# A gated mix of a long convolution and dilated attention: 114-query attention blocks, a second FFT stage in place, and whole-array weight loads

## The chip, the core and the metric

The kernel runs on one core of a Trainium2 chip. Five engines work side by side, each through its own instructions in order, and wait for one another on semaphores: TensorE (PE; its weight loads are listed apart as PEld), VectorE (DVE), ScalarE (ACT), GpSimd (POOL) and SyncE (SP, here the issuer of most DMAs). Matmul results go to PSUM, and VectorE or ScalarE copies them to SBUF. The metric is the device time of one execution in microseconds.

## What is computed

Inputs are bfloat16, with sequence S = 2048 and width D = 640. The same x (`A_q`) feeds a long convolution (a) and a windowed attention (b), mixed by a gate for each row.

```python
g = sigmoid((x * gate_w).sum(-1, keepdims=True))
# a: four-tap causal convolution of k, times v, then a 2048-tap causal convolution per channel
k_shift = sum(k_pad[:, t:t + S] * shift_k[:, 3 - t] for t in range(4))
kv = k_shift * v
a = x * (causal_conv(kv, ssm_k) + kv * ssm_D)          # by FFT of length 4096
# b: 32 heads of 20; a query at s sees the keys s, s-2, ..., s-14
q, k, v = split(x @ wqkv)
b = softmax(q . k_window * 20 ** -0.5) @ v_window @ wo
out = g * a + (1 - g) * b
```

## The kernel before

**Order.** The work is written as Python generators (`loads`, `conv`, `vproj`, `qkproj`, `score_gen` and so on), each of which yields requests for an engine with an estimated cost. A planner (`Plan.run`) picks among them by estimated start and priority while the program is built, and hands out four PSUM slots of two banks. The result is a fixed order of instructions on each engine; on the chip an engine never passes an instruction that waits.

**Attention.** Keys two apart have the same parity, so x is transposed (`transposes`) into `xT` with the even positions ahead of the odd ones, 1024 each, and the window becomes 8 neighbours. `vproj` (L440) makes the values `VW` for each block, with a 21st column of ones for the softmax's denominator. `qkproj` (L483) makes queries and keys for 128 features at a time in units of 10 matmuls; they are evicted to a staging tile `stg` (three buffers), and `fragger` (L524) sends the 20 rows of each head by DMA to row 32 x (head mod 4) of a set's tiles `qb` and `kb` (three of each; a set is four heads). Beneath the 20 feature rows lie 11 constant rows that add a large negative number to each score outside the window. A block is `BQ` = 57 queries against `BK` = 64 keys, 36 blocks. `score_gen` (L543) computes block scores with 31-row, 64-column tiles: two heads lie in each half of the 128 PSUM partitions. ScalarE takes the exponential (L567) into one of eight `ET` tiles, `pv_gen` (L587) multiplies by `VW`, and VectorE divides (L597, L601) into `oS`. Sets run t = 0 to 7.

**Convolution.** VectorE computes `kv` in 64 instructions of 1280 elements (L397 to L408). The long convolution is a four-step transform of 32 x 64 points: `s1h_unit` (L620) for the filter `h` and `s1u_unit` (L643) for kv are its first stage, `s2_unit` (L664) its second, with constants `F` and `G`. kv lies with 32 of its rows on each quarter of the partitions, so L643 works in 32x32 tiles with 64 columns. Stage 1 is evicted to `Am`, stage 2 from `Am` to `Hs` or `Up`. The channels run in `NG` = 5 groups of `IL` = 16 of every 80. VectorE multiplies the spectra (`mults`, L754 and L757: `Up` by `Hs`, and by `Hw`, which is `Hs` with its halves of partitions exchanged by DMA, `swaps`). `inverse1` (L771) and `final` (L856) are the inverse stages, through `Cm`.

**End.** `outproj` transposes `oS` into `oT` (L793) and multiplies by `wo` (L810) in tiles of 32 weight columns, four column groups side by side; the eviction scales by 1 - g into `bl`. `late_loads` reads x again into `qg` and the constants `T`; `qscale` (L836) multiplies by g. `final` runs twice, over groups 0 to 2 and then 3 and 4: VectorE multiplies the result in PSUM by `qg` (L863), adds `bl` (L867), and the output is stored in pieces of four rows to a partition block.

The two lines that set the sizes of a score and of an output matmul:

```python
nc.tensor.matmul(dst, lhsT=kb[r:r + DH + NF, BK * b:BK * b + BK], rhs=qb[r:r + DH + NF, BQ * b:BQ * b + BQ], ...
                 tile_position=(r, 64 * (rg // 2)))
nc.tensor.matmul(O[64 * sg:64 * sg + 64, half, c0:c0 + 21], lhsT=ET[64 * half:64 * half + 64, hl, BQ * (b % 8):BQ * (b % 8) + 64],
                 rhs=VW[64 * half:64 * half + 64, b, 2 * t + hl, :], ...)
```

Of the kernel before, what the change touches and what calls it, by code (L numbers as in the profile page):

```python
# [26 lines left out]
BQ = 57  # L27
BK = 64
NBP = 18
NB = 2 * NBP  # L30
PRE = 7
HS = 1024 + PRE
XW = 2072
# [4 lines left out]
OP = BQ * NBP  # L38
NET = 8


NG = 5
IL = 16
CR = 4

# [35 lines left out]
def attn_consts():  # L81
    B, C = 256.0, 512.0
    kk = np.arange(BK); qq = np.arange(BQ)
    kc = kk // 8 - 4; ko = kk % 8; qc = qq // 8 - 4; qo = qq % 8
# [19 lines left out]
def ccol(sb):  # L104
    return PRE + 128 * sb + (PRE if sb >= 8 else 0)
# [24 lines left out]
class Req:  # L130


    def __init__(self, engs, cost=0.0, deps=(), take=0, give=(), n=0, move=0.0, pri=None, mode=None, bg=None):
        self.engs, self.cost, self.deps, self.take, self.give, self.n, self.move = engs, cost, deps, take, give, n, move
        self.pri, self.mode, self.bg = pri, mode, bg
# [3 lines left out]
SWITCH = 110.0  # L139


class Plan:


    def __init__(self, nslots):
        self.at = dict(P=0.0, A=0.0, D=0.0, G=0.0, S=0.0, Q=0.0)
        self.mode = None
        self.pipe = 0.0
        self.lane = {"S": [], "G": [], "Q": []}
        self.slots = [Bank() for _ in range(nslots)]  # L150
        self.streams = []
        self.log = []
# [29 lines left out]
    def run(self):  # L182
        while self.streams:
# [13 lines left out]
            g.eng, g.banks = e, []  # L197
            g.done = Ev(end, e)
# [22 lines left out]
def kernel(  # L221
# [41 lines left out]
    kin = p0.tile([128, 35, 320], BF, name="kin", tag="H")  # L263
    kv = p0.tile([128, 32, 320], BF, name="kv", tag="kv")
    G = p0.tile([128, 32, 2, 128], BF, name="G")
    F = p0.tile([128, 384], BF, name="F")
    F1b = F[:, 0:128]
    M = F[:, 128:384].rearrange("p (a b) -> p a b", a=2)
    g_nat = p0.tile([128, 16], F32, name="g_nat")
# [4 lines left out]
    VW = pR.tile([128, NB, 16, DH + 1], BF, name="VW")  # L274
    ksets, qsets, ETs = [], [], []
    for e in range(3):
        kb = pR.tile([128, KW], BF, name=f"kb{e}")
        qb = pR.tile([128, QW], BF, name=f"qb{e}")
        ksets.append(kb); qsets.append(qb)
    for e in range(NET):  # L280
        ETb = pR.tile([128, 2, 8 * BQ + 8], BF, name=f"ET{e}")
        ETs.append(ETb)
    rd = pR.tile([128, 2, 12, 2], F32, name="rd")
# [4 lines left out]
    pa = pL.tile([128, CR, 320], BF, name="pa")  # L288
    wraw = pL.tile([128, 320, 4], BF, name="wraw", tag="pb")
    wl = pL.tile([128, 4, 320], BF, name="wl")  # L290
# [21 lines left out]
    st = {}  # L312
# [3 lines left out]
    def loads():  # L316
        def load(name, dst, src, us, deps=(), bg=None):
            g = yield Req("S", 500.0, deps, move=us, bg=bg, pri=None if bg is None else 6)
# [6 lines left out]
        def load_rows(name, dst, src, r0, r1, off):  # L325
            for rho in range(4):
                gg, ch = rho // 2, rho % 2
                lo = -3 if (r0 == 0 and off and gg == 1) else r0
                yield from load(f"{name}{rho}", dst[32 * rho:32 * rho + 32, lo + off:r1 + off, :],
                                raw(src, (32 * gg + lo) * D + 320 * ch, [[64 * D, 32], [D, r1 - lo], [1, 320]]),  # L330
                                (r1 - lo) * 32 * 640 / 200.0)
# [7 lines left out]
        yield from load_rows("kA", kin, k2, 0, 16, 3)  # L339
        yield from load("W0", Wqk[:, :, 0, :], W3[:, :, 0, :], 2400.0)  # L340
        yield from load_rows("vA", kv, v2, 0, 16, 0)
        yield from load("W1", Wqk[:, :, 1, :], W3[:, :, 1, :], 2400.0)
        yield from load_rows("kB", kin, k2, 16, 32, 3)
        yield from load_rows("vB", kv, v2, 16, 32, 0)
        wo = p0.tile([128, NDT, D], BF, name="wo", tag="wo")
        st["wo"] = wo
        yield from load("wo", wo[:], B_wo.rearrange("(t p) n -> p t n", p=128), 2400.0, [ev("vproj")], 500.0)
        for a in range(4):
            yield from load(f"G{a}", G[:, 8 * a:8 * a + 8], cf["G"].ap().rearrange("p (a r b) -> p a r b", a=32, r=2)[:, 8 * a:8 * a + 8],
                            1300.0, (), 500.0)  # L350
        h_lin = p0.tile([128, 80, 2, 64], BF, name="h_lin", tag="H")
        st["h"] = h_lin
        for c in range(2):
            for q in range(4):
                yield from load(f"h{q}{c}", h_lin[32 * q:32 * q + 32, :, c, :],
                                raw(A_ssm_k, (320 * c + 80 * q) * S, [[64, 32], [S, 80], [1, 64]]), 2100.0, [ev("conv")], 500.0)

    def heads():
        for c0, c1 in ((0, PRE), (HS, HS + PRE), (2 * HS, XW)):
            nc.gpsimd.memset(xT[:, :, c0:c1], 0.0)  # L360
        for ch in range(2):
            nc.gpsimd.memset(kin[32 * ch:32 * ch + 1, 0:3, :], 0.0)
        nc.scalar.dma_start(mm[:], ca["mm"].ap())
        for rho in range(4):
            nc.scalar.dma_start(wraw[32 * rho:32 * rho + 32], raw(A_shift_k, 1280 * (rho % 2), [[0, 32], [4, 320], [1, 4]]))
        for ch in range(2):
            for a, b in ((1, 17), (17, 32)):
                nc.scalar.dma_start(kin[32 * ch + a:32 * ch + b, 0:3, :],
                                    raw(k2, (64 * a - 3) * D + 320 * ch, [[64 * D, b - a], [D, 3], [1, 320]]))
# [3 lines left out]
        for q in range(4):  # L373
            nc.scalar.dma_start(Dz[32 * q:32 * q + 1, :], raw(A_ssm_D, 80 * q, [[0, 1], [320, 2], [1, 80]]))
        for e in range(3):
            nc.gpsimd.tensor_copy(ksets[e][:].rearrange("p (b k) -> p b k", k=BK), mm[:, 0:BK].unsqueeze(1).to_broadcast([128, NB, BK]))
            nc.gpsimd.tensor_copy(qsets[e][:].rearrange("p (b k) -> p b k", k=BQ), mm[:, BK:BK + BQ].unsqueeze(1).to_broadcast([128, NB, BQ]))
        nc.gpsimd.memset(VW[:, :, :, DH], 1.0)
        for o in (0, 64):
            for j in (0, NBP):  # L380
                nc.gpsimd.memset(VW[o:o + PRE, j, :, DH], 0.0)
        for e in range(NET):
            nc.gpsimd.memset(ETs[e][:], 1.0)
# [3 lines left out]
    def conv():  # L387
        yield Req("D", 1700.0, [Ev(12000.0)])
# [536 lines left out]
```

## Time and profile before

| | |
|---|---|
| median of 3 runs | 350.29 us (347.28 to 351.41) |
| the profiled execution | 352.19 us, of which the profile's span is 350.1 us |
| mean granted clock of TensorE in it | 0.817 |
| TensorE reads its first data | 6.9 us |
| first score matmul, first exponential | 62.5 us, 63.4 us |
| first matmul of the filter's transform (L620) | 165.0 us |
| first product of spectra (L754) | 217.8 us |
| projection (L810), first to last | 213.6 to 292.9 us |
| last VectorE instruction ends | 341.7 us |

All times below are microseconds from the start of the span. A row of the timeline or of the groups reads: line of the kernel, engine, operation, tile written, tiles read, shapes, count; in a timeline the start and the length stand ahead of it. The bracket or the last column says how long the engine had been idle just before and what ended that; "issue" is idle time in which the engine waited for nothing that the profile shows. In the slices each digit is a tenth of busy share (9 is 90% or more) and `PEclk` is the clock granted to TensorE in tenths. Matmuls are pipelined, so the durations of neighbours overlap; where the text speaks of a step, it is the distance between starts.

The largest idle times of the two engines that evict are ScalarE's 31.0 us for scores (L543) and 27.9 us for `pj` (L483), and VectorE's 38.0 us for outputs (L587).

### The profile page before, as it was taken

Reading aid. Unit: us, or ns where it says so; the run is one execution under the profiler, and the core shown is the slowest. Engines: PE = TensorE matmul, PEld = TensorE weight load, DVE = VectorE, ACT = ScalarE, POOL = GpSimd, SP = SyncE. Lnnn points to the kernel's source line nnn. Section 1 sums busy time; section 2 is a strip of 40 time slices with the busy share of each in tenths; the row PEclk is TensorE's granted clock in tenths of the full one; section 3 lists DMA queues with packets and bytes.
Section 4 is the critical chain, followed back from the end, with each engine's and each line's share of the span. In section 5 each row is a group of like instructions: output and inputs, shape, how many; then the busy total and the mean of one; then the engine's idle time right before and its main releaser. Section 6 shows DMA issues by size and latency. Waiting matters only on the chain. (4 is left out here: it accounts for less than half of the span.)

```text
span 350.1 us, 17133 instructions
## 1 busy us (share of the span) xinstructions
PE 251.0 (72%) x8158; PEld 198.0 (57%) x8158; DVE 176.1 (50%) x218; ACT 145.6 (42%) x172; POOL 24.7 (7%) x30
## 2 busy tenths in 40 slices
PE   2399999749599796465859788969979558445510
PEld 2278866646466464155748776947859436425510
DVE  0147699918574434113969552525434160996250
ACT  0235445604446354044767444736637424202200
POOL 9970000000000000001000000000000000000000
PEclk9999999958589898555787998998989977855855
DMA  7999964437323656173090000050501991000066
GB/s 202 272 217 221 220 139 102 84 107 195 108 75 81 126 103 108 31 132 63 7 222 22 5 6 4 4 124 4 123 5 33 235 203 78 6 4 2 4 152 150
DMA packets 39692, 34.78 MB, mean 99 GB/s; under 512 B 23246, under 2 KB 36552, under 8 KB 38472
## 3 DMA queue, kind: packets, MB, share of 16 engines
q1 hardware_dynamic: 38032, 31.82, 41.6%
q10 hardware_dynamic: 1592, 1.89, 2.5%
q8 instruction: 63, 1.03, 1.3%
q14 instruction: 5, 0.04, 0.0%
HBM read 20.26 MB, written 2.62 MB: 65 GB/s over the span
## 5 line engine op out<-in xcount | busy, mean ns | idle before, releaser
L483 PE MATMUL pj<-xT,Wqk 128*128 128x342 bf16 (+1 forms) x300 | 53.4, 340 | 2.3 <-issue 2.3
L567 ACT ACTIVATE ET<-sc 128x912 bf16<-128x912 f32 (+1 forms) x40 | 32.1, 853 | 31.2 <-PE sc L543 31.0
L483 PEld LDWEIGHTS <-Wqk 128*128 128x128 bf16 x300 | 30.4, 105 | 20.6 <-issue 2.4
L664 PE MATMUL s<-Am,G 64*128 64x64 bf16 x1280 | 30.3, 202 | 10.5 <-issue 8.2
L810 PE MATMUL op<-wo,oT 128*32 128x128 bf16 (+1 forms) x640 | 31.0, 349 | 8.2 <-issue 8.2
L664 PEld LDWEIGHTS <-G 64*128 64x128 bf16 x1280 | 25.8, 103 | 15.9 <-issue 12.0
L248 ACT CAST stg<-pj 128x684 bf16<-128x684 f32 (+1 forms) x25 | 19.0, 761 | 34.2 <-PE pj L483 27.9
L440 PE MATMUL psv<-Wv,xT 128*64 128x320 bf16 x360 | 28.1, 319 | 5.3 <-ACT xT L248 3.9
L248 ACT CAST Cm<-i 128x1024 bf16<-128x1024 f32 x17 | 17.2, 1012 | 26.2 <-PE i L771 26.1
L771 PE MATMUL i<-F,Hw 128*128 128x128 bf16 x160 | 24.0, 244 | 5.4 <-DVE Hw L757 5.4
L440 PEld LDWEIGHTS <-xT 128*64 128x64 bf16 x360 | 21.4, 117 | 11.0 <-ACT xT L248 4.4
L810 PEld LDWEIGHTS <-oT 128*32 128x32 bf16 x640 | 17.6, 142 | 17.0 <-issue 12.9
L754 DVE TENSOR_TENSOR Hs<-Up,Hs 128x2048 bf16<-128x2048 bf16 x10 | 12.2, 1222 | 27.2 <-ACT Up L248 27.1
L597 DVE RECIPROCAL rd<-O 128x48 f32<-128x48 f32 (+1 forms) x16 | 6.1, 383 | 38.4 <-PE O L587 38.0
L543 PE MATMUL sc<-qb,kb 31*64 31x57 bf16 x1152 | 17.9, 208 | 10.4 <-issue 5.8
L771 PEld LDWEIGHTS <-Hw 128*128 128x128 bf16 x160 | 21.9, 154 | 5.8 <-DVE Hw L757 5.6
L771 PE MATMUL i<-F,Hs 128*128 128x128 bf16 x160 | 24.4, 246 | 0.2 <-DVE Hw L757 0.2
L587 PE MATMUL O<-VW,ET 64*64 64x21 bf16 x1152 | 16.3, 191 | 10.7 <-issue 9.7
L543 PEld LDWEIGHTS <-kb 31*64 31x64 bf16 x1152 | 14.7, 124 | 16.1 <-issue 11.1
L643 PE MATMUL s1u<-F,kv 32*32 32x64 bf16 x1280 | 21.3, 217 | 3.5 <-issue 3.5
L771 PEld LDWEIGHTS <-Hs 128*128 128x128 bf16 x160 | 21.8, 153 | 1.4 <-issue 0.7
L643 PEld LDWEIGHTS <-kv 32*32 32x32 bf16 x1280 | 19.6, 144 | 5.2 <-issue 4.6
(55 smaller groups left out, 351.8 us busy)
## 6 DMA issues: line engine op xcount, KB each, us to landing
Hw<-Hs SPq DMA_DIRECT2D x10, 512.0 KB
xS<-in_A_q_dram SPq DMA_DIRECT2D x4, 640.0 KB
kv<-in_A_v_dram SPq DMA_DIRECT2D x8, 320.0 KB
h_lin<-in_A_ssm_k_dram SPq DMA_DIRECT2D x8, 320.0 KB
qg<-in_A_q_dram SPq DMA_DIRECT2D x4, 640.0 KB
kb<-stg SPq DMA_DIRECT2D x28, 90.0 KB
qb<-stg SPq DMA_DIRECT2D x28, 80.2 KB
G<-cf_G SPq DMA_DIRECT2D x4, 512.0 KB
```

The source lines that it names most:

```text
L248: nc.scalar.copy(dst, src)
L440: nc.tensor.matmul(ps[64 * o:64 * o + 64, i, 0:320], lhsT=xT[:, dt, s0:s0 + BK], rhs=rhs, start=(dt == 0), stop=(dt == NDT - 1), tile_posi ...
L483: nc.tensor.matmul(ps[:, i, 0:n], lhsT=Wqk[:, dt, w, 128 * ft:128 * ft + 128], rhs=xT[:, dt, s0:s0 + n], start=(dt == 0), stop=(dt == NDT ...
L543: nc.tensor.matmul(dst, lhsT=kb[r:r + DH + NF, BK * b:BK * b + BK], rhs=qb[r:r + DH + NF, BQ * b:BQ * b + BQ], start=True, stop=True, tile ...
L567: nc.scalar.activation(ETs[e][:, :, 0:BQ * nb], scs[k][:, :, 0:BQ * nb], ACT.Exp, scale=SCALE)
L587: nc.tensor.matmul(O[64 * sg:64 * sg + 64, half, c0:c0 + 21], lhsT=ET[64 * half:64 * half + 64, hl, BQ * (b % 8):BQ * (b % 8) + 64], rhs=V ...
L597: nc.vector.reciprocal(rv, Ov[:, :, :, :, DH])
L643: nc.tensor.matmul(pss[bank // 2][o:o + 32, bank % 2, 64 * k:64 * k + 64], lhsT=kv[rows, :, cp], rhs=F1b[rows, 64 * ch:64 * ch + 64], star ...
L664: nc.tensor.matmul(o, lhsT=G[rows, j, rr, :], rhs=Am[rows, 2 * j + rr, :, :], start=(rr == 0), stop=(rr == 1), tile_position=(64 * c, 0), ...
L754: nc.vector.tensor_tensor(Hs[:, c], Up[:, c], Hs[:, c], ALU.mult)
L771: nc.tensor.matmul(o, lhsT=src[:, c, :, :, 8 * oc + il].rearrange("p q j -> p (q j)"), rhs=M[:, k, :], start=(k == 0), stop=(k == 1), skip ...
L810: nc.tensor.matmul(op[32 * gg:32 * gg + 32, n0:n1], lhsT=raw(a, OP * (t % 2) + t // 2 + 8 * gg, [a.ap[0], [32, 32]]), rhs=wo[:, ft, n0:n1] ...
```

## The change

It rewrites most stages for fewer and larger matmuls. The number of matmuls, by line of before:

| | before | after |
|---|---|---|
| transposes of x (L420) | 80 | 80 |
| values (L440) | 360, 64-column weights | 180, 121-column weights |
| queries, keys (L483) | 300 | 300 |
| gate (L454) | 320 | 160 |
| scores (L543) | 1152, 57 columns | 576, 114 columns, 128-column weights |
| outputs (L587) | 1152 | 576 |
| stage 1 of h (L620) | 160 | 160 |
| stage 1 of kv (L643) | 1280, 32x32 tiles | 160, 64-row tiles with 128-column weights |
| stage 2 (L664) | 1280, 64 columns | 512, 160 columns |
| transposes of oS (L793) | 90 | 90 |
| projection (L810) | 640, 32-column weights | 160, 128-column weights |
| first inverse (L771) | 320 | 320 |
| last inverse (L856) | 1024, 96 or 64 columns | 512, 160 columns |
| all | 8158 | 3786 |

Attention blocks have 114 queries and 121 keys, 18 of them, and one head in a score tile; scores take two PSUM slots, and `stg` has two buffers.

```diff
-BQ = 57
-BK = 64
-NBP = 18
+BQ = 114
+BK = 121
+NBP = 9
+GROUPS = [[0, 1, 2, 3], [4, 5, 6, 7], [8, 9, 10, 11], [12, 13, 14], [15, 16, 17]]
+PARTS = [((0, 1, 2), 0, 2), ((3, 4), 12, 1)]
...
+            for gi, blocks in enumerate(GROUPS):
+                nb = len(blocks)
+                g = yield Req("P", 4 * nb * 28.0 + 30.0, [ev(f"set{t}"), ev("ET")], take=2, mode="s", mm=4 * nb)
...
+                for bb, b in enumerate(blocks):
+                    for rg in range(4):
+                        r = 32 * rg
+                        nc.tensor.matmul(scs[rg // 2][:, rg % 2, BQ * bb:BQ * bb + BQ], lhsT=kb[r:r + DH + NF, BK * b:BK * b + 128],
+                                         rhs=qb[r:r + DH + NF, BQ * b:BQ * b + BQ],
+                                         start=True, stop=True, tile_position=(r, 0), skip_group_check=True)
...
+                    nc.scalar.activation(st["ET"][0:BK, e, :, 0:BQ * nb], scs[k][0:BK, :, 0:BQ * nb], ACT.Exp, scale=SCALE)
...
+                                nc.tensor.matmul(O[:, (b - b0) // 6, c0:c0 + 21], lhsT=st["ET"][0:BK, e, hh, BQ * bb:BQ * bb + 128],
+                                                 rhs=VW[0:BK, b, 4 * t + h4, :], start=True, stop=True, skip_group_check=True)
...
-    CH = 6
+    NSTG = 2
```

kv is computed with 16 successive positions on each partition (instructions of 2560 elements), written to a tensor in memory, `kv_d`, and read back as `kvT`, so that both h and kv go through one first stage of 64 rows. `h`'s loads wait for the stores.

```diff
-    kv = p0.tile([128, 32, 320], BF, name="kv", tag="kv")
+    pv = p0.tile([128, 4, 2, 16, 80], BF, name="pv", tag="kv")
+    kv_d = dpool.tile([4, 128, 2, 16, 80], BF, name="kv_d")
...
+        for q in range(4):
+            yield from load(f"kvD{q}", kv_d[q].rearrange("p c n i -> p (c n i)"), pv[:, q].rearrange("p c n i -> p (c n i)"), 3000.0, [ev("conv")], 1500.0)
...
+    def s1_unit(key, P, oc, Am, free):
...
+                if key == "h":
+                    lhsT = st["h"][rows, i, :, :].rearrange("p c n -> p (c n)")
+                else:
+                    lhsT = st["kvT"][rows, :, :, i].rearrange("p c n -> p (c n)")
```

The channels run in two halves `P` instead of five groups. Stage 2 reads and overwrites the same tile (`Hs` or `U`); it can begin for a half only when stage 1 of that half is evicted. The first half of `h` needs no tile that attention holds, so its transform may begin during attention; the second half of kv reuses the tile of `oT` and follows the projection.

```diff
+    def s2_unit(j0, n, Am, deps):
+        r = yield Req("P", 4 * n * 34.0 + 30.0, deps + [ev(f"G{j // 8}") for j in (j0, j0 + n - 1)], take=1, mode="r", mm=4 * n)
...
+                    nc.tensor.matmul(ps[:, c, 160 * jj:160 * jj + 160], lhsT=st["G"][rows, j0 + jj, rr, :], rhs=Am[rows, :, 2 * (j0 + jj) + rr, :],
+                                     start=(rr == 0), stop=(rr == 1), tile_position=(64 * c, 0), skip_group_check=True)
...
+        copy(e.eng, Am[:, :, 2 * j0:2 * j0 + 2 * n, :].rearrange("p q (j c) l -> p c j q l", c=2),
+             ps[:, :, 0:160 * n].rearrange("p c (j q l) -> p c j q l", j=n, q=4))
...
+        yield Req("G", 1.0, [ev("outproj")])
+        U = p0.tile([128, 4, 64, PL], BF, name="U1", tag="H")
...
+            yield Req("S", 1.0, outs("h", P) + [ev("p3")] + ([ev("us1")] if P else []))
...
+                            nc.tensor.matmul(o, lhsT=src[:].rearrange("p q (j c) l -> p c l (q j)", c=2)[:, c, l + il, :], rhs=M[:, k, :],
```

The projection loads 128 weights at a time, the last inverse runs once over all 160 columns in groups of three rows (`m` = 3), and ScalarE copies its result to `yb` before VectorE multiplies and adds.

```diff
+                    nc.tensor.matmul(op[:, n0:n1], lhsT=oT[:, ft].rearrange("p h m a -> p a (h m)")[:, t, :], rhs=wo[:, ft, n0:n1],
...
+                nc.scalar.copy(yb[:, 0:m, 320 * k:320 * k + 320].rearrange("p n (q c) -> p q n c", q=2),
+                               pss[k][:, :, 0:160 * m].rearrange("p q (n c) -> p q n c", n=m))
...
+            nc.vector.tensor_tensor(reg, yb[:, 0:m, :], reg, ALU.mult)
...
+            nc.vector.tensor_tensor(reg, reg, bl[:, t0:t0 + m, :], ALU.add)
```

Inputs k and v are loaded in halves of 8 positions to a partition (10,240 bytes in a row), the taps on all 128 partitions, and one `ET` tile of eight parts is filled with ones after the first quarter of the convolution. The planner's costs get a term for each 256 instructions of TensorE (`PAGE`, `FETCH`); it changes the order, not the instructions.

## The prediction

> **What bounds the kernel now.** I read the page first (busy shares, slices, queues), then TensorE's timeline, then busy time by stage, then groups by form.
>
> ```profile
> PE 251.0 (72%) x8158; PEld 198.0 (57%) x8158; DVE 176.1 (50%) x218; ACT 145.6 (42%) x172; POOL 24.7 (7%) x30
> ...
> PE   2399999749599796465859788969979558445510
> ...
> PEclk9999999958589898555787998998989977855855
> ...
> q8 instruction: 63, 1.03, 1.3%
> ```
>
> TensorE is the busiest engine, 72% of the span, with holes from 60 us on, and its granted clock dips at the holes. The last line is the traffic of program code: 63 packets of 16 KB. TensorE has 16,318 instructions (8158 weight loads, 8158 matmuls, two branches); 256 to a packet makes 63.7. The timeline of TensorE in the last inverse transform shows what this does:
>
> ```profile
> 326.28 2.20 PE L856 MATMUL i<-Cm,T 32*32 32x64 bf16 x247 [1.10 <-ACT Cm L248]
> 330.54 1.29 PE L856 MATMUL i<-Cm,T 32*32 32x64 bf16 x128 [2.06 <-issue]
> 333.99 1.27 PE L856 MATMUL i<-Cm,T 32*32 32x64 bf16 x128 [2.17 <-issue]
> 337.75 0.26 PE L856 MATMUL i<-Cm,T 32*32 32x64 bf16 x9 [2.48 <-issue]
> ```
>
> Bursts of exactly 128 matmuls (256 instructions) run in 1.3 us and then wait for nothing else: one burst per 3.45 us (330.54 to 333.99), 27 ns a matmul where the array needs 10. My reading is that code arrives at 256 instructions per 3.45 us. Over all of TensorE's timeline "issue" waits come to 23.2 us from 62.5 to 165, 22.4 us from there to 298 and 10.3 us after: 56 us. By stage (columns: span, busy time and count of PE, PEld, DVE, ACT, POOL, clock, DMA share, GB/s):
>
> ```profile
> 16.00:62.50 46.50, 46.50 (x522) 34.63 (x519) 34.13 (x41) 21.75 (x31) 8.35 (x13) 1.00 0.91 181
> 62.50:165.00 102.50, 73.75 (x2817) 54.14 (x2816) 47.00 (x80) 43.21 (x56) 0.95 (x1) 0.73 0.49 102
> 165.00:298.00 133.00, 107.78 (x3655) 89.39 (x3652) 64.07 (x58) 73.18 (x78) 0.00 (x0) 0.87 0.31 71
> ```
>
> Projections fill the first stage at full clock. Attention, then the transforms, hold 2817 and 3655 matmuls; at 27 ns these need 76 of 102.5 us and 99 of 133 us for code alone. ScalarE comes next with 55% (73.18 of 133), so the code rate, with the low clock that its holes bring (0.73), is what these two stages are worth cutting for.
>
> **The change, stage by stage.** It issues 3786 matmuls: 7574 instructions, 102 us of code at 3.45 us per 256, spread over the whole span, so code stops being the bound everywhere but in the last transform.
>
> Prices that the trace has:
>
> ```profile
> L567 ACT ACTIVATE ET<-sc 128x912 bf16<-128x912 f32 x32 | 28.0, 928 | 20.8 <-PE sc L543 20.6
> L248 ACT CAST Cm<-i 128x1024 bf16<-128x1024 f32 x17 | 17.2, 1012 | 26.2 <-PE i L771 26.1
> L754 DVE TENSOR_TENSOR Hs<-Up,Hs 128x2048 bf16<-128x2048 bf16 x10 | 12.2, 1222 | 27.2 <-ACT Up L248 27.1
> 174.83 0.39 PE L620 MATMUL s<-F,h_lin 64*128 64x128 bf16 x8
> ```
>
> *To the first exponential (now 63.4 us).* ScalarE issues 10 loads ahead of its first copy instead of 15, so TensorE no longer stands until 15.8 us for xT; but its queue carries 0.69 MB more (taps on 128 rows, halo), 2.9 us at the 235 GB/s of the first 16 us, so Wv lands at 10.65 + 2.9 = 13.6 us. Then 60 transposes at 60 ns (3.6), 180 value matmuls at 136 ns (24.5: 1.36 us for 20 half-wide ones now, the same array time), 7 query/key units at 1.46 us (10.2) and 160 gate matmuls at 27 ns (4.3; the 320 of now take 10.7 us): 56.2, and 1 us for W0, now wanted earlier. **57 us.**
>
> *Attention (now 102.5 us).* Scores and outputs fall from 2304 matmuls to 1152. A score has a 128-column load and 114 columns on one of four row groups: bounds 12 ns (114 columns at the 0.42 ns of L483's 342 in 145, four abreast) and 64 ns (the 128x128 pairs of L771); nearest is L620 above, 8 matmuls with 128-column loads in 0.39 us, 27 ns apart once the pipe's 0.2 us is taken off. Outputs, 21 columns behind a full 128-column load: 11 (now) to 64, I take 35. So 15.6 + 20.2, 23 query/key units 33.6, and 9 us of first transforms: TensorE has 78 us. But ScalarE's exponentials double: 121 of 128 partitions hold one head where two shared them, so 48 of 912 columns and 32 of 684 replace 32 and 8. By the rows (0.928; 0.741 on the line through 0.554 at 456) that is 68.3 us, back to back (two in 1.75 us, a step of 0.82) 59.5; now 32.1. With 15 evictions of pj (11) and two of s1 ScalarE has 72 to 81 us and is the bound: I take 81, as its work mostly arrives in pairs.
>
> Waits on top: the convolution still takes 32 x 2 x 0.82 = 52 us of VectorE, from some 27 us (6.0 MB of loads up to k's first half at 225 GB/s) to 82 with the outputs of set 0 between. The new store of its product waits for that in SyncE's queue, ahead of the fragments for set 3, and two more 0.66 MB stores lie among them: at 220 GB/s the queries of the third feature block land near 92 us. With two staging buffers, not three, ScalarE's next eviction waits for these and blocks exponentials behind it, at about 85 us: 8 us. The same pair of buffers costs some 6 us in later sets (now 10.1 us of SyncE's waits on scores). Sum 81 + 14 = 95 us, to **152**. Bounds: 72 dense, 102.5 if nothing is won.
>
> *Transforms to the end of the projection (now 165 to 295).* The array needs 360 s2 matmuls at 35 ns (160/64 of 14 ns), 80 + 80 s1 at 27 and 45, 90 transposes at 56, 16 projection units at 1.4 (640 columns x 5 at 0.42 ns; four column groups abreast take 1.5 now), 160 L771 pairs at 64. Eviction bounds the first half: 30 on ScalarE at 0.9 (27 us, +2 for two barriers) against 21 on VectorE at 1.14 and 5 oT at 1.2 (30): **33 us**. Then TensorE has projection and inverse together, 22.4 + 10.2, at a clock near 0.9 **36 us**, covering VectorE's eight products (11.4) and bl (11.5). The strided weights (160-byte step, 32 now) are nowhere in the trace: 56 ns to twice 64 for L771 gives 32 to 43.
>
> *The last half (now 298 to 350 is 52).* It is serial: s1 for kv 7, meanwhile four swaps of 0.66 MB start only after its last matmul: 4.5 + 2.6 MB at 210 GB/s + 2 = 19, later than s2 (15). Then the products in 10, i1's last two units and a copy 4.5, code-and-VectorE-paced last transform 14.5 (11 products and sums at about 1.2, start and end), output 5 (8.4 us now for 1.3 MB behind the last sum; the last piece is 0.16 MB, behind 0.49 MB): **53 to 54**. Bounds 48 and 60.
>
> Sum: 57 + 95 + 33 + 36 + 54 = 275 us of span, and 2.1 outside it (352.19 against 350.1): 277 us. The profiled execution lies 1.9 us above the median of 350.29, inside the runs' 347.28 to 351.41; I leave it at 277.
>
> Done at no price: the ET fill (7 us on GpSimd, under the conv), the trip of kv to memory and back (2.6 MB each way, 12 us, under sets 5 to 7; if that cover is gone, up to 10 us before kv's s1), T and qg.
>
> Two rules stand against this. The Trainium skill, "Runtime: NRT & Kernel Launch", Instruction fetch mechanics, has the crossing of a 16 KiB block of code as mostly hidden; the four timeline rows with 2.1 to 2.5 us per block disagree, and by the page the 56 us would have another cause and stay, 333 us. "TensorE: Matmul & The Clock Gate", LDWEIGHTS, has 128 columns cost 107 ns a load, which would make the 1152 attention loads 123 us and the whole some 350; the row with 8 such loads in 0.39 us says a quarter.
>
> **Rivals.**
> - *Attention wins nothing* (102.5 us): doubled exponentials and blocked queues eat the code gain. For it: ScalarE runs in order and evicts pj between exponentials. 57 + 102.5 + 123 + 2 = 285, up to 308 with the upper bounds behind it.
> - *The stalls are not code* and stay with time: 277 + 56 = 333. Against: bursts of 128, and 63 packets.
> - *All dense*: 57 + 72 + 29 + 32 + 48 + 2 = 240 to 257.
> - *Slower: PSUM serializes attention.* There are four slots of two banks; a score group now takes two, outputs one, pj one. If exponentials, scores, outputs and pj of a set never overlap, a set costs 3 x 2.7 + 2 x 2.2 (scores, 0.25, two exponentials, 0.12), 3.7 + 2.2 for outputs and their division, and three pj units at 2.45: 25.8 us, eight sets 206, and the whole 388. It decides from 21.6 us a set, against 11.9 in my sum. For it: the first eight exponentials each wait for both slots; against: two slots stay for the other group whenever no pj or output is in flight.
>
> **Chances.** Forecast 0.60; attention wins nothing 0.19; dense 0.06; stalls stay 0.05; serialized 0.10, of which 0.02 come out within 1%. A change under about 1% can't be told from none here. Range 255 to 308, holding the first two cases. Faster 0.90, same 0.02, slower 0.08.
>
> **What would show it.** Code packets near 30 and "issue" waits of TensorE under 15 us, nearly all in the last transform; exponentials 60 to 68 us with few gaps between 57 and 152; ScalarE waiting for DMA on stg near 85 us; ScalarE and VectorE over 85% busy in the 33 us after attention; Hw late against U1. Wrong if the first exponential starts after 62, if a set takes over 15 us, or if L771's pairs with the new stride are over 100 ns apart.

## The result, and the profile after

The changed kernel takes 304.11 us, the median of 4 runs (302.72 to 305.58), beside 350.85 us for the kernel before (4 runs, 347.28 to 354.11): a ratio of 0.870, 95% interval 0.861 to 0.878. The time lies in the forecast range, 27 us above the forecast. The profiled execution took 305.58 us, 303.8 of it span. These lines of its page answer to those shown of before:

```profile
PE 231.9 (76%) x3781; PEld 185.7 (61%) x3786; DVE 172.5 (57%) x181; ACT 177.8 (59%) x217; POOL 24.5 (8%) x23
...
PE   0499999997988895994888979999999742984210
...
PEclk9999999859799799697555999999999795895555
...
q8 instruction: 29, 0.48, 0.7%
```

63 packets of code have become 29. TensorE is nearly full as far as the projection's end at 233 us, though with dips of its clock, and thin behind that. Busy time by stage (columns: span, busy time and count of PE, PEld, DVE, ACT, POOL, clock, DMA share, GB/s):

```profile
63.90:167.00 103.10, 84.74 (x1473) 56.38 (x1473) 49.78 (x67) 74.57 (x97) 0.94 (x1) 0.78 0.63 141
...
167.00:198.00 31.00, 27.63 (x611) 24.24 (x610) 29.18 (x29) 26.51 (x30) 0.00 (x0) 0.98 0.40 87
198.00:234.00 36.00, 35.69 (x327) 29.90 (x334) 16.87 (x25) 23.08 (x28) 0.00 (x0) 1.00 0.50 104
...
268.00:304.00 36.00, 9.96 (x545) 7.62 (x544) 12.56 (x12) 12.89 (x15) 0.00 (x0) 0.59 0.32 75
```

The last row is the sight to explain: 36 us in which no engine is busy for more than 13. By stage, in us of span:

| stage | before | forecast | after |
|---|---|---|---|
| to the first exponential | 63.4 | 57 | 63.9 |
| attention, to the last output matmul | 101.6 | 95 | 103.0 |
| transforms to the projection's start | } 133 | 33 | 31.0 |
| projection and first inverse, first half | } | 36 | 35.6 |
| the rest | 52.1 | 54 | 70.3 |

By these stages the whole gain came from the two in the middle (133 to 66.6); attention won nothing, and the last half lost 18 us. They do not hold the same work as before, though. Attention now also holds the start of the filter's transform (7.4 us of TensorE), and the last half holds the second half of kv's transform and half of the first inverse (25.0 us of TensorE, where 7.9 of such work stood before). A large part of what the last half lost is in ScalarE's timeline of the last transform:

```profile
277.04 0.88 ACTq L876 DMA_DIRECT2D out_dram<-qg  x2
277.97 1.82 ACT L866 CAST yb<-i 128x960 bf16<-128x960 f32 x2 [3.33 <-DVE qg L873]
282.20 0.86 ACTq L876 DMA_DIRECT2D out_dram<-qg  x2
283.16 1.82 ACT L866 CAST yb<-i 128x960 bf16<-128x960 f32 x2 [3.37 <-DVE qg L873]
```

Every 5.19 us ScalarE evicts a group of three rows (L866), then comes to the issue of that group's output DMAs (L876), which must wait for VectorE's sum (L873). The next group's evictions stand behind that issue: 3.4 us idle in each round. TensorE and VectorE in turn wait for the eviction, as the table of waits shows (us in total, times, longest):

```profile
DVE qg L871 <- ACT yb L866: 23.1, 6, 10.0
ACT yb L866 <- DVE qg L873: 16.8, 5, 3.4
...
PE i L859 <- ACT yb L866: 7.9, 5, 3.1
```

In the kernel before, VectorE multiplied out of PSUM itself, and none of the last transform's evictions stood behind ScalarE's DMA issues.

### The profile page after: what moved, and what is told of

It is laid out like the page before. It is cut to its first block, busy times and chain, and to the rows that moved or that the text cites. A ratio compares the mean times of both kernels' runs of the same rounds, so it can differ in the third digit from the quotient of the medians.

```text
span 303.8 us, 8436 instructions
## 1 busy us (share of the span) xinstructions
PE 231.9 (76%) x3781; PEld 185.7 (61%) x3786; DVE 172.5 (57%) x181; ACT 177.8 (59%) x217; POOL 24.5 (8%) x23
## 4 chain that ended last, share of the span: by engine, by line
PE 58%; DVE 17%; DMA 9%; ACT 6%; SPq 4%; issue 4%; ACTq 1%; DVEq 0%
PE pj L522 14%; PE i L777 9%; PE psv L476 9%; PE op L810 7%; PE O L617 5%; DVE U L269 5%; DVE Hs L269 4%; DMA Hw<-Hs 4%; DMA xS<-in_A_q_dram 3%; PE sc L589 3%; PE gps L494 3%; SPq L563 2%; PE s L669 2%; DMA kb<-stg 2%; DVE qg L871 2%
## 5 line engine op out<-in xcount | busy, mean ns | idle before, releaser
L597 ACT ACTIVATE ETall<-sc 121x912 bf16<-121x912 f32 (+1 forms) x80 | 63.4, 858 | 22.2 <-PE sc L589 21.9
L476 PE MATMUL psv<-Wv,xT 128*121 128x320 bf16 x180 | 28.7, 313 | 1.0 <-DVE xT L269 1.0
L269 DVE CAST U<-s 128x1024 bf16<-128x1024 f32 (+2 forms) x23 | 25.8, 1171 | 6.0 <-PE s L669 3.2
L589 PE MATMUL sc<-qb,kb 31*128 31x114 bf16 x576 | 20.2, 243 | 10.7 <-DMA kb<-stg 3.7
L267 ACT CAST stg<-pj 128x684 bf16<-128x684 f32 (+1 forms) x21 | 15.6, 745 | 18.7 <-PE pj L522 14.3
L476 PEld LDWEIGHTS <-xT 128*121 128x121 bf16 x180 | 24.9, 142 | 2.5 <-issue 1.2
L267 ACT CAST Hs<-s 128x960 bf16<-128x960 f32 (+1 forms) x25 | 23.1, 994 | 3.1 <-PE s L669 1.8
L269 DVE CAST Hs<-s 128x1024 bf16<-128x1024 f32 (+2 forms) x17 | 19.1, 1152 | 7.6 <-PE s L653 6.1
L810 PE MATMUL op<-wo,oT 128*128 128x512 bf16 (+1 forms) x155 | 22.6, 301 | 0.3
L267 ACT CAST VW<-psv 121x640 bf16<-121x640 f32 x18 | 12.5, 696 | 14.6 <-PE psv L476 14.6
L866 ACT CAST yb<-i 128x960 bf16<-128x960 f32 (+1 forms) x12 | 9.9, 873 | 18.0 <-DVE qg L873 16.8
L810 PEld LDWEIGHTS <-oT 128*128 128x128 bf16 x160 | 16.5, 147 | 5.9
```

The costliest lines, as they stand in the source:

```text
L267: nc.scalar.copy(dst, src)
L269: nc.vector.tensor_copy(dst, src)
L476: nc.tensor.matmul(ps[0:BK, n0 // 320, 0:320], lhsT=xT[:, dt, s0:s0 + BK], rhs=Wv[:, dt, n0:n1], start=(dt == 0), stop=(dt == NDT - 1))
L589: nc.tensor.matmul(scs[rg // 2][:, rg % 2, BQ * bb:BQ * bb + BQ], lhsT=kb[r:r + DH + NF, BK * b:BK * b + 128], rhs=qb[r:r + DH + NF, BQ * ...
L597: nc.scalar.activation(st["ET"][0:BK, e, :, 0:BQ * nb], scs[k][0:BK, :, 0:BQ * nb], ACT.Exp, scale=SCALE)
L810: nc.tensor.matmul(op[:, n0:n1], lhsT=oT[:, ft].rearrange("p h m a -> p a (h m)")[:, t, :], rhs=wo[:, ft, n0:n1], start=(ft == 0), stop=(f ...
```

## The experiments

All ratios are to the kernel before, timed on the same chip. "The changed kernel" is the 304 us one.

**Outputs issued by SyncE alone.**

```diff
-                (nc.sync, nc.scalar)[gg % 2].dma_start(raw(outf, ...
+                nc.sync.dma_start(raw(outf, ...
```

> The changed kernel, but all four output DMAs of a group of rows are issued by SyncE; before, two of four were issued by ScalarE. Theory: in the changed kernel's last transform ScalarE's DMA issue waits for VectorE's sum of that group, and as ScalarE works in order the next group's two evictions stand behind it; a group takes 5.19 us and the transform 28.8 us (271.7 to 300.5). With SyncE issuing, a group costs the largest of its code (96 matmuls, 0.75 of a 3.45 us packet, 2.6 us), ScalarE's two evictions of 960 elements (about 2 us) and VectorE's product and sum (about 2.4 us): 2.6 us a group, the transform 15 to 17 us, the whole 12 us less: about 292 us. Rival A, the transform is bound by code or by VectorE anyhow: a group stays near 5 us and the time within 3 us of 304. Rival B, eight DMA issues on one queue in place of two queues cost the gain back at the end: about 300 us.

297.21 us (4 runs, 295.91 to 298.72), ratio 0.845 (0.837 to 0.853), clear of the changed kernel's interval. ScalarE's and VectorE's timelines in the last transform now read:

```profile
281.23 3.55 ACT L866 CAST yb<-i 128x960 bf16<-128x960 f32 x4 [1.84 <-PE i L859]
285.36 2.48 ACT L866 CAST yb<-i 128x960 bf16<-128x960 f32 x4 [0.58 <-PE i L859]
```

```profile
285.36 1.15 DVE L871 TENSOR_TENSOR qg<-yb,qg 128x1920 bf16<-128x1920 bf16 x1
286.54 1.16 DVE L873 TENSOR_TENSOR qg<-qg,bl 128x1920 bf16<-128x1920 bf16 x1
287.62 1.15 DVE L871 TENSOR_TENSOR qg<-yb,qg 128x1920 bf16<-128x1920 bf16 x1
```

Evictions run four in a row, and VectorE goes at its own pace, 2.26 us a group. From the transform's first matmul to its last sum it takes 17.9 us, where it took 28.8. SyncE's 24 issues end 2.7 us behind the last sum, so the tail grew from 3.3 to 5.0 us; with a start 1.3 us later the span is 7.9 us shorter. The mechanism is shown; I had expected 12 us of it.

**Code in the kernel before: each score matmul issued twice.**

```diff
                             score(scs[sl][o:o + 64, rg % 2, BQ * k:BQ * k + BQ], rg, 16 * a + 8 * sl + k)
+                            score(scs[sl][o:o + 64, rg % 2, BQ * k:BQ * k + BQ], rg, 16 * a + 8 * sl + k)
```

> The kernel before, with every score matmul issued twice with the same operands into the same place, so 1152 matmuls and 1152 weight loads more, all in attention; the result is the same. Theory (TensorE's program code arrives at 256 instructions per 3.45 us and this bounds attention): 2304 instructions are 9 packets, 63 become 72, and attention gets up to 9 x 3.45 = 31 us longer: about 375 to 382 us. Rival, the stalls come from something else and the array's time counts: a score matmul of 57 columns is at most 11 ns busy beside others, 1152 x 11 = 13 us, part of it in holes: 350 to 363 us.

380.74 us (4 runs), ratio 1.081 (1.068 to 1.094). Its page:

```profile
q8 instruction: 72, 1.18, 1.4%
```

The scores' waits in it, and below them those of the kernel before:

```profile
PE sc L543 <- issue: 18.4, 12, 2.3
```

```profile
PE sc L543 <- issue: 5.8, 4, 2.0
```

Nine packets more, and a span of 376.1 in place of 350.1 us: 2.9 us a packet, near the 3.45 of the bursts. About half of it is in these waits, the rest in TensorE's busy time (251.0 to 266.8 us); the rival, the array's time alone, had allowed 13 us at most. The code rate did bound attention before. The Trainium skill, "Runtime: NRT & Kernel Launch", Instruction fetch mechanics, has the crossing of such a block as mostly hidden; these 26 us for nine blocks say otherwise.

**Attention: half of the exponential's columns.**

```diff
-... activation(st["ET"][0:BK, e, :, 0:BQ * nb], scs[k][0:BK, :, 0:BQ * nb], ACT.Exp, scale=SCALE)
+... activation(st["ET"][0:BK, e, :, 0:57 * nb], scs[k][0:BK, :, 0:57 * nb], ACT.Exp, scale=SCALE)
```

> The changed kernel, with each exponential taken over half of its columns only (57 a block in place of 114); the other half of the weights stays as it was, so part of the softmax is left out. The forecast had ScalarE as the bound of attention with 81 us of work out of 95. The 80 exponentials are 63.4 us now and would be about 36. Theory (ScalarE bounds attention): attention shortens by most of 27 us, the whole to 277 to 283 us. Rival A (attention stands on staging buffers, on fragment DMAs and on TensorE's order, ScalarE busy only 63 of 95 us): it shortens by 5 to 12 us, the whole to 292 to 299 us. Rival B (nothing but TensorE's order): within 4 us of 304.

305.15 us in one run: nothing won. ScalarE is busy 48.1 us of attention in place of 74.6, and attention is 2.2 us shorter.

**Attention: three of five feature blocks in the query and key projections.**

```diff
-                        for dt in range(NDT):
+                        for dt in (0, 2, 4):
```

> The changed kernel, with the query and key projections summed over three of the five blocks of 128 input features; two fifths of that sum are left out, everything behind it is issued as before. 120 of 300 projection matmuls of 342 to 349 columns are gone. With the exponentials halved nothing was won, so ScalarE does not bound attention. Theory (TensorE's own work in order bounds it, 84.6 us busy of 103): 21 us fall in the 103 us after the first exponential (150 ns for 126 of the matmuls, as most of the projections stand there) and 2 to 3 us before it: about 280 to 287 us. Rival (the fragment DMAs behind stores and loads in SyncE's queue bound it): the waits for kb and qb grow by what the matmuls give up, and the whole is 296 to 304 us.

301.15 us in one run, and attention 4.2 us shorter, where 21 had been expected: TensorE's work does not bound it either. Part of the missing matmuls was paid back by the clock. Busy time by stage of this run:

```profile
82.00:95.00 13.00, 9.53 (x177) 6.09 (x177) 6.17 (x9) 9.14 (x12) 0.00 (x0) 0.58 0.63 193
...
125.00:140.00 15.00, 8.18 (x186) 5.93 (x182) 5.67 (x9) 9.92 (x14) 0.94 (x1) 0.62 0.83 206
```

The granted clock in these windows is 0.58 and 0.62; in the changed kernel it is 1.00 and 0.92. Over attention TensorE's busy time fell by 10.1 us (84.7 to 74.6), not by the 15 that the 92 missing matmuls at 165 ns (ten in 1.65 us at full clock) are.

**Attention: the filter loaded in long runs.**

```diff
-                yield from load(f"h{q}{c}", h_lin[32 * q:32 * q + 32, :, c, :], raw(A_ssm_k, ..., [[64, 32], [S, 80], [1, 64]]), ...
+                yield from load(f"h{q}{c}", h_lin[32 * q:32 * q + 32, 40 * c:40 * c + 40]..., raw(A_ssm_k, ..., [[5120, 32], [1, 5120]]), ...
```

> The changed kernel, with the filter h_lin loaded as eight pieces of 10 KB runs a row in place of runs of 128 bytes: the same bytes and the same eight issues, but the filter's elements come in another order, so that branch computes something else. Halved exponentials and two fifths fewer projections each won at most 4 us, so neither ScalarE nor TensorE sets the pace of attention. Theory (the 16 DMA engines do, 0.63 to 0.84 busy from 82 to 152 us, with 21,448 packets under 512 bytes of which 20,480 are this load): the DMA share there falls below 0.5, TensorE's 3.7 and 3.2 us of waits for kb shrink, and the whole is 4 to 10 us less: 294 to 300 us. Rival (SyncE's issues do, 0.75 us for a fragment, some 61 of the 70 us from 82 to 152; or the turns of TensorE, VectorE and four PSUM slots do): within 2 us of 304, although the share falls.

304.41 us (4 runs), ratio 0.869 (0.863 to 0.875): no change. The DMA share from 125 to 140 us fell from 0.83 to 0.63, and attention by 2.2 us; a lead of 2.8 us at the last output matmul was 1.1 at the end of the span. Small packets on the DMA engines are not the bound.

**All three together**, the last three edits in one kernel.

> The changed kernel with three edits at once: exponentials over half of their columns, query and key projections over three of five feature blocks, the filter loaded in 10 KB runs; half of the exponentials and two fifths of the projection's sum are left out, and the filter's elements come in another order. Alone they shortened attention (first exponential to the last output matmul, 103.0 us) by 2.2, 4.2 and 2.2 us. Theory (no single engine's work bounds it: TensorE, ScalarE, VectorE, SyncE's issues and the PSUM slots hand on to each other in a written order, and TensorE's clock falls where the projections thin out): the three add to little more than 9 us, attention is 92 to 96 us, and the last three sets, which have no projection, stay at 10.4 us each. Rival (two near-equal bounds, ScalarE and TensorE, of which each alone hides the other): attention falls by 18 us or more, to 80 to 85 us.

299.0 us in one run. First exponential, end of the last output matmul, and what lies between:

| | first | last | between | TensorE busy | ScalarE busy | clock |
|---|---|---|---|---|---|---|
| changed kernel | 63.93 | 166.96 | 103.0 | 84.7 | 74.6 | 0.78 |
| exponentials halved | 64.27 | 165.07 | 100.8 | 83.6 | 48.1 | 0.77 |
| projections 3/5 | 60.38 | 159.16 | 98.8 | 74.6 | 73.9 | 0.69 |
| filter in long runs | 63.30 | 164.14 | 100.8 | 83.3 | 74.4 | 0.79 |
| all three | 60.87 | 156.43 | 95.6 | 70.8 | 48.1 | 0.73 |

The savings nearly add (2.2, 4.2 and 2.2 to 7.4) and stay small; the rival of two bounds hiding each other had asked for 18 or more. TensorE's timeline of the run with all three shows the last sets:

```profile
129.81 1.03 PE L653 MATMUL s<-F,h_lin 64*128 64x128 bf16 x16 [6.59 <-POOL h_lin L680]
132.15 1.45 PE L617 MATMUL O<-VW,ETall 121*128 121x21 bf16 x48
...
142.55 1.46 PE L617 MATMUL O<-VW,ETall 121*128 121x21 bf16 x48
...
152.93 1.43 PE L617 MATMUL O<-VW,ETall 121*128 121x21 bf16 x48 [0.37 <-DVE Hs L269]
```

Each set takes 10.4 us (132.15, 142.55, 152.93), as in the changed kernel (142.49, 152.90, 163.26), though the exponentials are halved. In these sets the scores wait in turn for VectorE and ScalarE to free PSUM slots (`DVE oS`, `DVE Hs` and `ETall` end TensorE's idle times in the changed kernel). But these waits are the smaller part of a set: TensorE is busy for 8.2 of the 10.4 us here and for 8.5 in the changed kernel, at a granted clock of 0.50, and none of the three edits takes work from it in these sets. Whether its own work at half clock or the hand-overs set the 10.4 us was not tested. The first row is a second fixed point: the filter's transform stands in TensorE's order ahead of the scores and waits for the filter, whose loads are queued on SyncE behind the stores of kv and among the fragments. That wait is 3.2 us in the changed kernel and 6.6 here, so it takes back part of what is won ahead of it.

**Attention: other issuers.** In the first of these GpSimd issues the stores of kv and the loads of the filter and of G; in the second it issues the fragments of the keys.

```diff
-            nc.sync.dma_start(dst, src)
+            (nc.gpsimd if name[0] == "h" or name[:3] == "kvD" or name[0] == "G" else nc.sync).dma_start(dst, src)
```

> The changed kernel, with the store of kv's product, the loads of the kernel's filter (h_lin) and of G issued by GpSimd, so that the query and key fragments no longer stand behind them in SyncE's queue. Theory (queue order: 5.2 us of VectorE, 3.9 of ScalarE and 6.9 of TensorE wait for fragments between 84 and 141 us): TensorE's 3.7 and 3.2 us go, the forecast's 8 us near 85 with them, and the whole is 4 to 9 us less: 295 to 300 us. Rival A (the 16 DMA engines themselves are the limit, 0.63 to 0.84 busy there, with 21,448 packets under 512 bytes): the fragments share the engines with the loads and come no sooner: within 2 us of 304. Rival B (GpSimd takes long to issue them, or its loads come ahead of the fragments): h_lin or fragments late, 306 to 315 us.

```diff
-                    nc.sync.dma_start(dst[r0:r0 + rows, 0:wd], stg[fa - f0:fb - f0, 0:wd])
+                    (nc.gpsimd if w else nc.sync).dma_start(dst[r0:r0 + rows, 0:wd], stg[fa - f0:fb - f0, 0:wd])
```

> The changed kernel, with the fragments of the keys issued by GpSimd and those of the queries still by SyncE, as are all stores and loads; the instructions of TensorE, VectorE and ScalarE stay in the same order. Theory (SyncE's issues set the pace: 0.75 us a fragment, 32 key fragments of 85 KB, 24 us of its 61 from 82 to 152): TensorE's 3.7 and 3.2 us of waits for kb go and VectorE's 5.2 for qb, the whole is 4 to 10 us less: 294 to 300 us. Rival A (the DMA engines set it): within 2 us of 304. Rival B (GpSimd's own issue is slow, 1.2 us each in the run that gave it the bulk loads, and bulk loads now run ahead of the fragments): 304 to 312 us. Rival C (turns through four PSUM slots at 10.4 us a set, as in the last three sets): within 3 us of 304 even though the waits for fragments shrink.

Both are slower than the changed kernel: 316.98 us, ratio 0.904 (0.896 to 0.912), and 314.97 us, ratio 0.899 (0.892 to 0.905). In the first the stores and six of the eight filter loads are issued within 10 us of 82, and fill the DMA engines before the fragments. By stage, and in the waits:

```profile
82.00:95.00 13.00, 5.73 (x65) 3.42 (x64) 0.47 (x3) 4.77 (x6) 9.35 (x10) 0.86 0.95 282
```

```profile
DVE stg L269 <- DMA kb<-stg: 22.7, 2, 15.1
```

DMA share 0.95, TensorE busy 5.7 of 13 us, and VectorE waiting 22.7 us for a staging buffer. So the queue in which fragments stood behind bulk loads had also kept the bulk loads off the fragments. The second run shows the like later (DMA share 1.02 from 140 to 152 us), and whether GpSimd's issue or the bulk loads running ahead cost more there is not separated. SyncE's issue rate as the bound of attention therefore stays untested. A third staging buffer was not tried.

**First inverse: weights from 128 contiguous columns.**

```diff
-... lhsT=src[:].rearrange("p q (j c) l -> p c l (q j)", c=2)[:, c, l + il, :], rhs=M[:, k, :],
+... lhsT=src[:].rearrange("p q x l -> p (q x l)")[:, 128 * il:128 * il + 128], rhs=M[:, k, :],
```

> The changed kernel, with the weights of the first inverse stage read as 128 contiguous columns in place of 128 columns 160 bytes apart; it reads other elements of the same tile, so that stage computes something else. Theory: the step costs about 20 ns a matmul (83 to 86 ns a matmul now, 64 in the kernel before with a step of 32 bytes): 320 matmuls, the last 160 of them alone on the path, 3 to 7 us less, 297 to 301 us. Rival: the matmul time is the 128-column load and the clock, whatever the step: under 1 us.

321.82 us, ratio 0.914 (0.906 to 0.922): the whole got slower, since the columns now read cross the pieces that several products write. From 198 to 275 us TensorE's waits for `Hs` are 16.2 us in place of 8.6, and VectorE now waits 10.4 us for TensorE to have read `Hw`. The time says nothing on the step, but the timelines do. The changed kernel, then this run, both at a granted clock of 1.00 (start, length):

```profile
205.01 0.25 PE L777 MATMUL i<-F,Hs 128*128 128x128 bf16 x1
205.09 0.25 PE L777 MATMUL i<-F,Hw 128*128 128x128 bf16 x1
205.18 0.25 PE L777 MATMUL i<-F,Hs 128*128 128x128 bf16 x1
```

```profile
211.76 0.22 PE L777 MATMUL i<-F,Hs 128*128 128x128 bf16 x1
211.81 0.22 PE L777 MATMUL i<-F,Hw 128*128 128x128 bf16 x1
211.87 0.22 PE L777 MATMUL i<-F,Hs 128*128 128x128 bf16 x1
```

Starts are 83 ns apart with the 160-byte step and 56 without, 27 ns less. That holds at full clock only: where the granted clock is 0.50 (from 257 us in the changed kernel, from 264 us here), both are 107 ns apart, so the step does not cost this on all 320 matmuls.

**The swapped copy's room**, with the outputs from SyncE.

```diff
-            yield Req("S", 1.0, outs("h", P) + [ev("p3")] + ([ev("us1")] if P else []))
+            yield Req("S", 1.0, outs("h", P) + [ev("p3")] + ([ev("i10")] if P else []))
...
-            Hw = ... if P == 0 else st["p2"].tile([128, 4, 64, PL], BF, name="Hw", tag="kvT")
+            Hw = ... if P == 0 else p0.tile([128, 4, 64, PL], BF, name="Hw", tag="kv")
```

> The run that issues all outputs from SyncE, and with it the swapped copy of the second half of the filter's spectrum in the room of the first half's, so that it need not wait for the last kv first stage, but only for the first half's inverse. Theory: its four DMAs are issued from about 217 us and not from 238.5, land by 236, and VectorE's products start when U's second stage is out (248.7), not at 253.3: 4.5 us less, 292 to 293 us. Rival A: the first half's inverse ends with the projection (233.5), not earlier, and the swap gains nothing: 297 us. Rival B: its DMAs collide with the loads of the query and of T at 210 to 228: less than 2 us gained.

289.56 us (4 runs, 287.57 to 291.6), ratio 0.8245 (0.8175 to 0.8314), clear of the run with the outputs alone. In the changed kernel VectorE's first product of the second half waits for the swap; here, below, it does not:

```profile
253.33 1.76 DVE L760 TENSOR_TENSOR Hs<-U,Hs 128x3072 bf16<-128x3072 bf16 x1 [5.79 <-DMA Hw<-Hs]
```

```profile
248.05 1.76 DVE L760 TENSOR_TENSOR Hs<-U,Hs 128x3072 bf16<-128x3072 bf16 x1
```

The swap is issued at 218.4 in place of 238.5, and the products start 6.2 us before those of the run with the outputs alone (254.27).

**Taps, halo and F behind x**, with the outputs from SyncE. The planner's estimate of when the convolution can start goes from 12 to 16 us with it.

```diff
-        nc.scalar.dma_start(wraw.rearrange("p c j -> p (c j)"), raw(A_shift_k, 0, [[0, 128], [1, 4 * D]]))
-        for a, b in ((1, 113), (113, 128)):
-            nc.scalar.dma_start(halo[a:b].rearrange("p n c -> p (n c)"), raw(k2, (16 * a - 3) * D, [[16 * D, b - a], [1, 3 * D]]))
-        nc.scalar.dma_start(F[:], cf["F"].ap())
...
         yield from load_x(3)
+        nc.sync.dma_start(wraw.rearrange("p c j -> p (c j)"), raw(A_shift_k, 0, [[0, 128], [1, 4 * D]]))
...
+        nc.sync.dma_start(F[:], cf["F"].ap())
```

> The run that issues all outputs from SyncE, and with it the taps, the halo rows and F (0.75 MB) issued by SyncE behind the four loads of x, and no longer by ScalarE ahead of all. Theory: x's first part lands 2 to 4 us earlier than 10.9 us and Wv before 14.2, ScalarE's table load begins before 14.0; TensorE's first stage starts 3 us earlier and as TensorE works almost without a hole to the first exponential (63.9) the whole is 2 to 4 us less: 293 to 295 us. Rival A: ScalarE's table load still stands at the issue of the last small DMA, so its first copy comes at 15 us, and the start is unchanged: 297 us. Rival B: the convolution starts later by the same 3 us and drags the product's store and the fragments with it: 297 to 300 us.

293.9 us (4 runs), ratio 0.836 (0.829 to 0.842). The interval overlaps that of the outputs alone, so the time does not settle the gain; the timelines bear it out. TensorE's first rows, the changed kernel and this run:

```profile
10.93 2.32 PE L458 MATMUL trx<-ident,xS 128*128 128x128 bf16 x20 [10.93 <-DMA xS<-in_A_q_dram]
14.22 4.81 PE L476 MATMUL psv<-Wv,xT 128*121 128x320 bf16 x20 [0.98 <-DVE xT L269]
```

```profile
7.29 2.31 PE L458 MATMUL trx<-ident,xS 128*128 128x128 bf16 x20 [7.29 <-DMA xS<-in_A_q_dram]
10.59 5.25 PE L476 MATMUL psv<-Wv,xT 128*121 128x320 bf16 x20 [0.98 <-DVE xT L269]
```

It is 3.6 us earlier at the start. Against the run with the outputs alone it is 2.7 us earlier at the first exponential (60.72 against 63.42) and 4.3 at the last output matmuls.

**The three that won, together**: outputs from SyncE, the swapped copy's room, taps and halo behind x.

> The changed kernel with the three edits that won time together: outputs issued by SyncE alone, the second swapped copy in the room of the first half's spectrum, taps, halo and F issued behind the loads of x. Alone they gave 7 (304.1 to 297.2), 7.6 (to 289.6) and 3.3 us (to 293.9) in ratios to the kernel before of 0.870, 0.845, 0.824 and 0.836. Theory (they lie in different stages and add): 0.824 less 0.010 is 0.814 to 0.816 of the kernel before, 286 us. Rival: the earlier start is lost in attention, whose pace is set elsewhere: 289 to 290 us.

286.85 us (6 runs, 284.09 to 289.51), ratio 0.816 (0.810 to 0.822): faster than both kernels, and as forecast if the gains add. Its interval overlaps that of outputs and swap without the taps (0.8175 to 0.8314), so the part of the taps in it is not clear of the noise.

## Why the forecast came out as it did

*Code* was a right reason. There are 29 packets against "near 30"; TensorE's matmuls wait for "issue" only in the last transform (3.7 us at L859, where the kernel before has 56 in all), and the run with the doubled scores prices a packet in attention. For the two stages that won it is in part argued. Of their 66 us the waits for "issue" were 22.4; TensorE's busy time fell by 45 more (107.8 to 63.0), through fewer and wider matmuls and through work that moved to other stages, and no run puts code back there.

*To the first exponential* (57, measured 63.9) three terms were too small. The extra 0.69 MB was charged to Wv alone, but x landed late as well (10.93 us, 6.9 before), and value matmuls began at 14.2 rather than 13.6. The first 20 of them took 4.65 us, where 20 later ones take 2.72. And "160 gate matmuls at 27 ns", 4.3 us, took 9.0: 56 ns each. One of the forecast's own signs of being wrong came true here: the first exponential starts after 62.

*Attention* (95, measured 103.0): the step that failed is "ScalarE has 72 to 81 us and is the bound". Its work was sized well (74.6 us), but taking 26 us of it away gave 2.2. That the size came out near is luck: the same stage has another limit of much the same height. The runs leave two candidates for it: hand-overs in a written order, through four PSUM slots and two staging buffers, and TensorE's own work at a clock that falls in this stage (0.78 over it, 0.50 in the last sets). How much each of them holds is not settled. The rival "attention wins nothing", given 0.19, is what this stage did. That PSUM serializes it (25.8 us a set) is out: a set takes 12.9.

*Transforms and projection* (33 and 36, measured 31.0 and 35.6) held. In the first, eviction is the bound as forecast (VectorE busy 29.2 of 31 us), though the terms given add up to 30 and not 33. The 36 is partly luck: the clock was 1.00 and not "near 0.9", while the first inverse took 13.4 us of TensorE and not 10.2, as its matmuls are 83 ns apart and not 64.

*The last half* (54, measured 70.3) holds the largest miss. The swap was right (19 us to its landing, 19.7 measured). From there the products and "i1's last two units and a copy" took 3.9 us longer than the 14.5 forecast. The products did not set the pace (they end at 264.6); the first inverse did, its 160 matmuls 107 ns apart at a clock of 0.50 up to 260.4 and 80 ns apart behind that, in place of 64. The bound for strided weights had allowed for it. The "code-and-VectorE-paced last transform 14.5" took 28.8: I costed the engines' work and left out that ScalarE now both evicts and issues half of the output DMAs. The run with SyncE as the only issuer takes 10.9 us of these 14.3 back; the rest is in part code: its first groups come 3.5 us apart and TensorE waits 5.4 us for "issue" there.

So the sign and the times of the middle stages were right, and the sum was low by 28.8 us of span: 6.9, 8 and 16.3 in these three stages, less 2.4 in the two that held. That the time still lies in the forecast range is owed to its upper end, which was drawn for the rival "attention wins nothing".

## What to carry to other kernels

A DMA issue that waits for another engine belongs on a queue with nothing urgent behind it: on an evicting engine it holds up the next eviction, and no row of busy time shows that; the table of waits and a steady period in the timeline do. Cutting instructions pays where code arrives too slowly and nothing else stands close behind: attention was bound by code, lost nearly half of its matmuls and won nothing. So count packets by stage, and look for the next limit there, before crediting the whole span. When one engine's work is cut and the stage does not move, cut a second and then both: savings that only add, and stay small, speak against two bounds that hide each other. What does set the pace, the order of hand-overs or an engine whose work was left alone, still has to be found.

## What the runs showed of the hardware

The granted clock falls without long idle times, and even without any. The gate's 160 matmuls of one column run behind the value projections, 56 ns apart:

```profile
54.32 9.01 PE L494 MATMUL gps<-wg,xT 128*64 128x1 bf16 x160
```

```profile
57.00:64.00 7.00, 7.00 (x133) 6.71 (x132) 6.86 (x6) 0.07 (x1) 0.00 (x0) 0.65 0.23 84
```

TensorE is busy all the time here (7.00 of 7.00 us), yet the clock goes from 1.00 to 0.50 at 59.1 us; the matmuls stay 56 ns apart. Later it goes to 0.50 at 141 us, behind a wait of 3.2 us, and stays there up to 168 us, although TensorE is 84% busy from 152 to 167 us (12.5 of 15) and its longest wait there is 0.7 us. In the run with thinned projections it falls at 84.2 us, where the longest wait shortly before was 1.8 us. The Trainium skill, "TensorE: Matmul & The Clock Gate", HAM oscillation, puts the rule as no idle gaps over some 3.4 us; here the clock fell with shorter gaps and with none. The first stretch is all matmuls of one column, and the one up to 168 us mostly of 21, 114 and 128; that this is the cause was not tested.

A weight load of 128 columns with its matmul of 128 columns costs by the step of the weights at full clock: 80 to 83 ns at 160 bytes, 56 contiguous. At a clock of 0.50 both cost 107. DMAs issued by GpSimd appear on a queue of their own kind (`q0 software_dynamic`), and in both runs that used it the kernel was 11 to 13 us slower than the changed kernel; how much of that is the queue and how much the changed order of transfers is not separated.
